# A third score buffer for the first batch of a hashed attention kernel, and the preparation work moved around it

## The chip, the cores and the metric

The kernel runs on one core of one Trainium2 chip. The metric is the device time of one execution in microseconds (us). The profile's span, from the first to the last instruction, is 1.7 to 1.9 us shorter in every execution of the kernel before. Engines are PE (TensorE matmul), PEld (its weight load), DVE (VectorE), ACT (ScalarE), POOL (GpSimd) and SP (SyncE); a name ending in q is an engine's issuing side. L290 is line 290 of the kernel that the trace belongs to, so the same code has different numbers before and after.

## The reference

Attention in which a query sees only keys of the same hash bucket (six sign bits of a projection), then a layer `h * cos(h)` between two matrices.

```python
# q, k, v: (4, 8, 768, 64)   proj: (64, 6)   w_in: (512, 2048)   w_out: (2048, 512)
q_bits = (einsum('bhsd,dk->bhsk', q, proj) > 0)      # k_bits likewise
mask   = q_bucket[:, :, :, None] == k_bucket[:, :, None, :]   # bucket = the bits as a number
scores = where(mask, q @ k.T / sqrt(64), -1e9)
attn   = softmax(scores)                             # denominator + 1e-9
x      = (attn @ v) -> (3072, 512)                   # heads side by side
h      = x @ w_in
out    = (h * cos(h)) @ w_out
```

## The kernel before

The mask costs no separate step: Q and K get six further rows of signs times a constant, so that one matmul gives score plus bonus for equal bits, and an exp with a fixed bias makes the rest vanish. A *unit* is one head and one block of 128 keys: two score matmuls, one exp on ScalarE, six value products. There are 48 units in a batch and 192 in all. After unit 55 comes the first layer of batch 0, after 103 that of batch 1, and so on. Batches 1 to 3 have the second layer of an earlier batch to fill TensorE between units (`fill`); batch 0 has nothing.

Two heads are a *pair*, 16 pairs in all. Each needs, ahead of its first score: loads, casts (GpSimd), block transposes (VectorE), the hash (TensorE), signs, and Q and K with tokens along the free dimension. Pairs 0 to 4 get the last by TensorE transposes and copies out of an output bank; the others by a transposing transfer that gives Q, and a VectorE copy (`k_copy`) that moves K to its own tile.

```python
s_ps = [psp.tile([P, 2, 512], FP32, name=f"s_ps{i}") for i in range(2)]   # two scores, 2 banks each
av_ps = [psp.tile([P, 512], FP32, name=f"av_ps{i}") for i in range(2)]    # two value banks
m_ps = [psp.tile([P, 512], FP32, name=f"m_ps{i}") for i in range(2)]      # two output banks
...
def score(h, jt):
    sp = s_ps[state["rot"] % 2]
    ...                                   # two matmuls, then the exp
def kc(n=n):
    k_copy(n, 0); k_copy(n, 1); bits_dma(n, (0, 1, 2, 3))
...
# preparation of pair n (n >= 5), s0 = 12 * (n - 1) - 6 (pair 5: - 4)
at(s0 - 1, lambda n=n: load(n + 1, nc.gpsimd))      # pairs 7 to 14
at(s0, start)       # casts, block transposes
at(s0 + 2, hsh)     # transposing transfers
at(s0 + 3, hsh2)    # hash, signs, bit rows (pair 5: s0 + 5)
at(s0 + 7, kc)      # K copies, bit rows to Q and K
...
for u in range(U):
    score(h, jt); pend.append((h, jt))
    ...  av_step()                        # value products; after a head's last: normalisation
    for f in acts.get(u, ()): f()         # the preparation placed at unit u
    ...  fill(UF(u))
```

The order in the program is each engine's order. What matters later: `kc` at unit 121 comes *behind* that unit's value products, and so behind the normalisation of the head that ends there.

The softmax here doesn't subtract the row's maximum and nothing guards it: scores larger than these inputs give would overflow.

Of the kernel before, what the change touches and what calls it, by code (L numbers as in the profile page):

```python
# [9 lines left out]
FP32 = mybir.dt.float32  # L10
# [12 lines left out]
def kernel(  # L23
# [31 lines left out]
    GDEF = range(2)  # L55
    COOL = False

    glob = ctx.enter_context(tc.tile_pool(name="glob", bufs=1))
# [21 lines left out]
    warm = glob.tile([P, 1], FP32, name="warm")  # L80
    wz = glob.tile([P, 512], FP16, name="wz")
    proj2 = glob.tile([32, 2, NBITS], FP32, name="proj2")
    projblk = glob.tile([P, 2, 4, 8], FP32, name="projblk")
# [6 lines left out]
    vs_bufs = [glob.tile([P, 2, W], FP16, name=f"vs{i}") for i in range(3)]  # L90

    s_ps = [psp.tile([P, 2, 512], FP32, name=f"s_ps{i}") for i in range(2)]
    av_ps = [psp.tile([P, 512], FP32, name=f"av_ps{i}") for i in range(2)]
    m_ps = [psp.tile([P, 512], FP32, name=f"m_ps{i}") for i in range(2)]
    state = {"m": 0, "rot": 0, "hold": False, "cool": False}

# [48 lines left out]

    def blocks(pr, hh=None):
        if pr not in blk:
            blk[pr] = [blkp.tile([P, 2, T, 2, 32], FP32, name=nm) for nm in ("blkq", "blkk")]
        for w in range(2):
            if hh is None:  # L150
                nc.vector.transpose(  # L151
                    out=blk[pr][w].rearrange("p h t c r -> p (h t c r)"),
                    in_=nat[pr][w].rearrange("p h f -> p (h f)"))
            else:
                nc.vector.transpose(
                    out=blk[pr][w][:, hh].rearrange("p t c r -> p (t c r)"),
                    in_=nat[pr][w][:, hh])
# [87 lines left out]
    pts = {}  # L245

    def score(h, jt):
        pr, hh = divmod(h, 2)
        sp = s_ps[state["rot"] % 2]
        state["rot"] += 1  # L250
        for c, (c0, c1) in enumerate(((0, 512), (512, 768))):
            nc.tensor.matmul(  # L252
                out=sp[:, c, 0:c1 - c0],
                lhsT=kx(pr)[:, hh, jt * P:(jt + 1) * P],
                rhs=qx(pr)[:, hh, c0:c1],
                start=True, stop=True)
        pt = ptp.tile([P, S], FP16, name="pt")
        nc.scalar.activation(  # L258
            out=pt, in_=sp.rearrange("p c n -> p (c n)")[:, 0:S], func=ACTF.Exp,
            bias=exp_bias, scale=EXP_SCALE)  # L260
        pts[(h, jt)] = pt

    def av(h, jt):
        pr, hh = divmod(h, 2)
        bank = av_ps[h % 2]
        if jt == 0 and h < DPE:
            nc.tensor.matmul(
                out=bank[:, 0:T * W].rearrange("p (t w) -> p t w", w=W)[:, :, 0:D + 1],
                lhsT=delta_w,
                rhs=vs_bufs[pr % 3][:, hh, 0:D + 1].unsqueeze(1).to_broadcast([P, T, D + 1]),  # L270
                start=True, stop=False, skip_group_check=True)
        elif jt == 0:
            nc.tensor.matmul(
                out=bank[:, T * W:T * W + D + 1], lhsT=delta_w, rhs=vs_bufs[pr % 3][:, hh, 0:D + 1],
                start=True, stop=False, skip_group_check=True)
        pt = pts.pop((h, jt))
        for qt in range(T):
            nc.tensor.matmul(  # L278
                out=bank[:, qt * W:qt * W + D + 1],
                lhsT=pt[:, qt * P:(qt + 1) * P],  # L280
                rhs=vx_bufs[pr % 3][:, hh, jt, 0:D + 1],
                start=False, stop=(jt == T - 1 and qt == T - 1), skip_group_check=True)

# [25 lines left out]
    def xtrans(b, ft):  # L309
        xT[(b, ft)] = xtp.tile([P, T, P], FP16, name=f"xT{ft}")  # L310
        nc.sync.dma_start_transpose(
            out=xT[(b, ft)], in_=xn[(b, ft)].rearrange("p t w d -> p (t w d)"))

    g_tiles = {}
# [83 lines left out]
    def av_step():  # L398
        ph, pj = pend.pop(0)
        av(ph, pj)  # L400
        if pj == T - 1:
            norm(ph)
            if ph % 2 == 1:
                xtrans(ph // H, (ph % H) // 2)

    def warmup(n):
        for _ in range(n):
            nc.tensor.matmul(  # L408
                out=s_ps[1][:, 1, :], lhsT=wz[:, 0:P], rhs=wz, start=True, stop=True,
                skip_group_check=True)  # L410

    with tc.manual_schedule():

        nat[0] = [natp.tile([P, 2, T * D], FP32, name=nm) for nm in ("natq", "natk", "natv")]
        aps = [heads_ap(src, 0) for src in (q, k, v)]
        nc.scalar.dma_start(out=proj2, in_=proj.rearrange("(c p) i -> p c i", c=2))
        nc.sync.dma_start(out=nat[0][0][:, 0], in_=aps[0][:, 0])
        nc.scalar.dma_start(out=nat[0][1][:, 0], in_=aps[1][:, 0])
        nc.sync.dma_start(out=nat[0][0][:, 1], in_=aps[0][:, 1])
        nc.sync.dma_start(out=nat[0][1][:, 1], in_=aps[1][:, 1])  # L420
        nc.scalar.dma_start(out=nat[0][2], in_=aps[2])
        load(1, nc.sync)
        load(2, nc.sync)
        nc.vector.memset(wz, 0.0)
        nc.vector.memset(exp_bias, EXP_BIAS)
        nc.vector.memset(cos_bias, math.pi / 2.0)
        nc.vector.memset(projblk, 0.0)
        nc.vector.memset(bitrow, 2.0 * BIT)
# [12 lines left out]
        warmup(8)  # L441
        for b_ in range(4):
            nc.vector.tensor_copy(
                out=projblk[32 * b_:32 * b_ + 32, :, b_, 0:NBITS], in_=proj2)
        blocks(0, 0)
        cast_qk(0, 0, (nc.scalar, nc.scalar))
# [10 lines left out]
        warmup(1)  # L457
        rows_copy(nc.vector, pe_transposes(0, 0, 1, av_ps[0]))
        rows_copy(nc.scalar, pe_transposes(0, 0, 0, m_ps[0], range(0, 3)))
        rows_copy(nc.vector, pe_transposes(0, 0, 0, m_ps[1], range(3, 6)))  # L460
        blocks(0, 1)
# [9 lines left out]
        U = 2 * NP * T  # L471
        L1_AT = {UB * b + 7: b - 1 for b in range(1, B)}
        acts = {}

        def at(u, f):
            acts.setdefault(u, []).append(f)

        at(0, second_a)
        at(1, second_b)
        for w_ in range(2):  # L480
            at(2 + w_, lambda w_=w_: rows_copy(nc.vector, pe_transposes(0, 1, w_, m_ps[w_])))
        for n in range(1, NP):
            s0 = 12 * (n - 1) - (0 if n < NEARLY else 4 if n == NEARLY else 6)
            def start(n=n):
                cast_qk(n, None, (nc.gpsimd, nc.gpsimd))
                blocks(n)
                cast_v(n)
            if n < NEARLY:
                at(s0 + 2, lambda n=n: load(n + 2, nc.sync if n + 2 < NEARLY else nc.gpsimd))
            elif NEARLY + 1 < n < NP - 1:  # L490
                at(s0 - 1, lambda n=n: load(n + 1, nc.gpsimd))
            if n < NEARLY:
                o_ = 3 if n == 1 else 0
                held = {}
                def hash_a(half, n=n, held=held):
                    ts = range(3 * half, 3 * half + 3)
                    held["bh"] = hash_sums(
                        n, m_ps[half], [(j % 2, j // 2, ts) for j in range(4)],
                        held.get("bh"), 3 * half)
                def hash_b(n=n, held=held):  # L500
                    token_bits(n, held["bh"], m_ps[0])
                def trp(hh, w, n=n):
                    rows_copy(nc.vector, pe_transposes(n, hh, w, m_ps[1 - w]))
                at(s0 + o_, start)
                for half in range(2):
                    at(s0 + 3 + o_ + half, lambda hash_a=hash_a, half=half: hash_a(half))
                at(s0 + 5 + o_, hash_b)
                for i in range(4):
                    at(s0 + (6 if n == 1 else 7) + o_ + i, lambda trp=trp, i=i: trp(i // 2, i % 2))
            else:  # L510
                def hsh(n=n):
                    dma_transposes(n, 0)
                    dma_transposes(n, 1)
                def hsh2(n=n):
                    hash_mm(n, m_ps[1 - state["m"]])
                def kc(n=n):
                    k_copy(n, 0)
                    k_copy(n, 1)
                    bits_dma(n, (0, 1, 2, 3))
                at(s0, start)  # L520
                at(s0 + 2, hsh)
                at(s0 + (5 if n == NEARLY else 3), hsh2)
                at(s0 + 7, kc)
        for i in range(4):
            at(6 + 8 * i, lambda i=i: weights_in(i))

        done = 0
        for u in range(U):
            h, jt = divmod(u, T)
            score(h, jt)  # L530
            pend.append((h, jt))
            for _ in range(2):
                if len(pend) > (4 if u < T else 2):
                    av_step()
            for f in acts.get(u, ()):
# [4 lines left out]
            if u in L1_AT:  # L540
                bb = L1_AT[u]
                state["hold"] = bb > 0
                for ff in range(NFF):
# [8 lines left out]
                    if bb == 0:  # L552
# [5 lines left out]
                        elif ff == NFF // 2:  # L558
                            load(NEARLY + 2, nc.gpsimd)
                    if ff in AVS[bb > 0] and len(pend) > 0:  # L560
                        av_step()
# [49 lines left out]
```

## Time and profile before

| | before |
|---|---|
| time, median of 3 | 310.24 us (310.15 to 310.26) |
| first exp | 9.26 us |
| end of the batch-0 exps (start of the cosine table load) | 59.86 us |
| attention of batch 1, of batch 2 (between table loads) | 44.74, 44.56 us |
| K copies waiting for transposing transfers, whole span | 0.7 us |

ScalarE loads a table whenever it turns from exp to cosine or back, so the starts of those loads cut the span into stages. I compare stages so throughout. The lines of the profile are in the prediction below. Read the busy share of TensorE (97%) with suspicion, and the timeline of ScalarE in batch 0 as the real account: each new row there is a gap.

### The profile page before, as it was taken

The page shows a single profiled execution, that of the slowest core. Times are in us where ns is not written, and L with a number is a line of the kernel's source. Part 1 is how long each engine was busy: PE and PEld are TensorE (multiplying, and loading weights), DVE is VectorE, ACT ScalarE, POOL GpSimd, SP SyncE. Part 2 cuts the span into 40 slices and gives each one's busy share as a digit, 9 for nine tenths or more (in the row PEclk, how much of TensorE's full clock was granted, in tenths as well). Part 3 has the DMA queues.
Part 4 walks back from the last instruction along what each step waited for, and adds up shares of the span by engine and source line. Part 5 has one row for each costly group of instructions (what it writes and reads, how often), then busy time and mean ns, then how long its engine had stood idle before and what let it go on. Part 6 is the DMA issues. An engine that isn't in the chain of part 4 may idle for free.

```text
span 308.4 us, 7711 instructions
## 1 busy us (share of the span) xinstructions
PE 300.1 (97%) x3090; PEld 182.8 (59%) x3090; DVE 201.8 (65%) x434; ACT 234.3 (76%) x288; POOL 109.4 (35%) x180
## 2 busy tenths in 40 slices
PE   8899999899999999999999999999999999999995
PEld 3577677556566666555566666555566664565444
DVE  3665466877598988866777878766777343577211
ACT  3788999977899999766899999766899993577000
POOL 4898258378384684400064584100030000000000
PEclk9999999999999999999999999999999999999998
DMA  6969969289469856700169979200133223100121
GB/s 205 376 109 163 333 86 214 33 140 192 163 172 268 215 162 168 217 2 0 45 80 234 234 146 199 48 18 2 53 62 89 68 62 94 36 0 0 62 76 69
DMA packets 45332, 37.74 MB, mean 122 GB/s; under 512 B 32264, under 2 KB 39200, under 8 KB 45296
## 3 DMA queue, kind: packets, MB, share of 16 engines
q1 hardware_dynamic: 38080, 19.35, 28.9%
q0 software_dynamic: 6576, 17.17, 21.0%
q10 hardware_dynamic: 640, 0.72, 0.7%
q8 instruction: 24, 0.39, 0.5%
q14 instruction: 12, 0.10, 0.1%
HBM read 27.26 MB, written 6.29 MB: 109 GB/s over the span
## 4 chain that ended last, share of the span: by engine, by line
PE 89%; ACT 6%; DVE 3%; issue 1%; ACTq 0%; DVEq 0%
PE m_ps L370 26%; PE s_ps L320 18%; PE s_ps L252 18%; PE av_ps L278 10%; PE m_ps L320 6%; ACT pt L258 5%; PE m_ps L164 4%; PE av_ps L320 2%; PE s_ps L408 1%; PE m_ps L354 1%; PE m_ps L224 1%; DVE g L337 1%; DVE blkq L151 1%; ACT cos L332 1%; PE av_ps L164 1%
## 5 line engine op out<-in xcount | busy, mean ns | idle before, releaser
L258 ACT ACTIVATE pt<-s_ps,exp_bias 128x768 f16<-128x768 f32 x192 | 161.7, 899 | 11.1 <-PE s_ps L252 9.7
L370 PE MATMUL m_ps<-wout,g 128*128 128x512 f16 x368 | 105.6, 379 | 0.1
L252 PE MATMUL s_ps<-qx,kx 128*128 128x512 f16 (+1 forms) x384 | 93.8, 326 | 2.6 <-ACT pt L258 1.2
L278 PEld LDWEIGHTS <-pt 128*128 128x128 f16 x1152 | 58.7, 97 | 21.7
L320 PEld LDWEIGHTS <-win 128*128 128x128 f16 x512 | 50.0, 98 | 34.6 <-issue 0.2
L278 PE MATMUL av_ps<-vx,pt 128*128 128x65 f16 x1152 | 65.7, 193 | 0.0
L320 PE MATMUL s_ps<-xT,win 128*128 128x384 f16 x352 | 62.3, 326 | 0.1
L337 DVE TENSOR_TENSOR g<-s_ps,cos 128x768 f16<-128x768 f32 x44 | 42.1, 958 | 28.1 <-ACT cos L332 28.1
L332 ACT ACTIVATE cos<-s_ps,cos_bias 128x768 f16<-128x768 f32 x44 | 39.7, 901 | 26.8 <-PE s_ps L320 25.4
L252 PEld LDWEIGHTS <-kx 128*128 128x128 f16 x384 | 35.2, 97 | 31.1 <-issue 3.3
L138 POOL CAST vx<-natv 128x768 f16<-128x768 f32 x16 | 13.3, 829 | 92.8 <-PE av_ps L278 87.8
L370 PEld LDWEIGHTS <-g 128*128 128x128 f16 x368 | 31.2, 98 | 20.1 <-issue 3.3
L376 DVE COPY ob<-m_ps 128x512 f32<-128x512 f32 x23 | 15.8, 686 | 22.6 <-PE m_ps L370 22.6
L320 PE MATMUL m_ps<-xT,win 128*128 128x384 f16 x120 | 27.6, 326 | 0.0
L332 ACT ACTIVATE cos<-m_ps,cos_bias 128x384 f16<-128x384 f32 x30 | 16.3, 578 | 7.0 <-PE m_ps L320 7.0
L305 DVE TENSOR_TENSOR xn<-tot,rc 128x384 f16<-128x384 f32 x24 | 20.1, 839 | 0.8
L337 DVE TENSOR_TENSOR g<-m_ps,cos 128x384 f16<-128x384 f32 x30 | 15.7, 550 | 1.3 <-ACT cos L332 1.0
L300 DVE COPY dv<-av_ps 128x65 f32<-128x65 f32 x24 | 5.1, 211 | 16.9 <-PE av_ps L278 16.9
L140 POOL TENSOR_TENSOR vhalf<-natv 128x384 f32<-128x384 f32 x16 | 15.9, 996 | 0.0
L133 POOL CAST n16x<-natq 128x768 f16<-128x768 f32 (+1 forms) x16 | 13.1, 822 | 5.1 <-DMA natq<-in_q_dram 5.1
L133 POOL CAST n16x<-natk 128x768 f16<-128x768 f32 (+1 forms) x16 | 13.0, 813 | 5.5 <-DMA natk<-in_k_dram 5.5
L151 DVE STREAM_TRANSPOSE blkq<-natq 128x768 f32<-128x768 f32 x15 | 14.6, 975 | 0.3
(77 smaller groups left out, 274.8 us busy)
## 6 DMA issues: line engine op xcount, KB each, us to landing
out_dram<-ob SPq DMA_DIRECT2D x23, 256.0 KB
natq<-in_q_dram POOLq DMA_DIRECT2D x11, 384.0 KB, 3.9
natk<-in_k_dram POOLq DMA_DIRECT2D x11, 384.0 KB, 4.7
natv<-in_v_dram POOLq DMA_DIRECT2D x11, 384.0 KB, 5.7
win<-in_moe_w_in_dram POOLq DMA_DIRECT2D x4, 512.0 KB, 7.3
wout<-in_moe_w_out_dram POOLq DMA_DIRECT2D x16, 128.0 KB, 5.1
natq<-in_q_dram SPq DMA_DIRECT2D x4, 384.0 KB
natk<-in_k_dram SPq DMA_DIRECT2D x4, 384.0 KB
```

The source lines that it names most:

```text
L133: engs[w].tensor_copy(out=o_, in_=i_)
L140: nc.gpsimd.tensor_tensor(out=half, in0=nv[:, :, 0:3, :], in1=nv[:, :, 3:6, :], op=ALU.add)
L151: nc.vector.transpose(out=blk[pr][w].rearrange("p h t c r -> p (h t c r)"), in_=nat[pr][w].rearrange("p h f -> p (h f)"))
L252: nc.tensor.matmul(out=sp[:, c, 0:c1 - c0], lhsT=kx(pr)[:, hh, jt * P:(jt + 1) * P], rhs=qx(pr)[:, hh, c0:c1], start=True, stop=True)
L258: nc.scalar.activation(out=pt, in_=sp.rearrange("p c n -> p (c n)")[:, 0:S], func=ACTF.Exp, bias=exp_bias, scale=EXP_SCALE)
L278: nc.tensor.matmul(out=bank[:, qt * W:qt * W + D + 1], lhsT=pt[:, qt * P:(qt + 1) * P], rhs=vx_bufs[pr % 3][:, hh, jt, 0:D + 1], start=Fal ...
L305: nc.vector.tensor_tensor(out=dst, in0=tot[:, :, 0:D], in1=rc.unsqueeze(2).to_broadcast([P, T, D]), op=ALU.mult)
L320: nc.tensor.matmul(out=halves[c][:, 0:C2], lhsT=win_t[ft][:, ff * P:(ff + 1) * P], rhs=xT[(b, ft)][:, 3 * c:3 * c + 3, :], start=(ft == 0) ...
L332: nc.scalar.activation(out=c_, in_=h_, func=ACTF.Sin, bias=cos_bias, scale=1.0)
L337: nc.vector.tensor_tensor(out=g_, in0=h_, in1=c_, op=ALU.mult)
L370: nc.tensor.matmul(out=o_ps, lhsT=g[:, qt * P:(qt + 1) * P], rhs=wout_t[ff], start=(ff == 0), stop=(ff == NFF - 1))
L376: nc.vector.tensor_copy(out=ob, in_=o_ps)
```

## The change

The intent: in batch 0 nobody uses the output banks except hashes and transposes. If those go to the value bank that is idle at the time, the two output banks can be a third score buffer until the first layer, and TensorE may run one exp ahead. To fit this in, the preparation is placed by hand, in half units (a half unit means: ahead of that unit's value products). From unit 15 to 46 the value products also run three units behind the scores instead of two (`LAG`). The rest is a faster start and moved loads. The core of the diff:

```diff
+    third = psc.tile([P, 2, 512], FP32, name="s_ps2")     # released before the first layer
+    s_ps.append(third)
...
     def score(h, jt):
-        sp = s_ps[state["rot"] % 2]
+        if h * T + jt == N3:                               # N3 = 15
+            ...
+        sp = s_ps[state["rot"] % (2 if h * T + jt < N3 else len(s_ps))]
...
-            if ph % 2 == 1:
+            if ph % 2 == 1 and ph != H - 1:
                 xtrans(ph // H, (ph % H) // 2)
...
-        nc.scalar.dma_start(out=proj2, in_=proj...)        # and four copies to projblk
+        for b_, eng in enumerate((nc.scalar, nc.sync, nc.scalar, nc.sync)):
+            eng.dma_start(out=projblk[32 * b_:32 * b_ + 32, :, b_, 0:NBITS], in_=proj...)
...
-                at(s0 - 1, lambda n=n: load(n + 1, nc.gpsimd))      # s0 = 12 (n-1) - 6
+                at(s0 - 5, lambda n=n: load(n + 1, nc.gpsimd))      # s0 = 12 (n-1)
...
-                at(s0, start); at(s0 + 2, hsh); at(s0 + 3, hsh2); at(s0 + 7, kc)
+                units = LATE.get(n, [s0 - 6 + d_ for d_ in (0, 2, 3, 6.5)])   # start, hsh, hsh2, kc
+            if n % 4 == 2 and n > NEARLY + 1:
+                ...                        # casts, blocks, transfers inside the layer
+                at(s0 - 4 + HS, hsh2); at(s0 - 1.5, kc)
+        at(XPE, lambda: xtrans_pe(0, NFT - 1, av_ps[(H - 1) % 2]))  # last block of batch 0 by TensorE
...
+            for f in acts.get(u - 0.5, ()): f()            # ahead of the value products of u
```

In the same units as before: the loads were placed one unit ahead of the casts of the pair before, and are now one unit behind them; the K copies of pairs 8, 11, 12 and 15 were at a full unit (121 for pair 11) and are now half a unit earlier (120.5); those of pairs 10 and 14 are 2.5 units earlier, and those of pairs 9 and 13 now stand inside a first layer.

## The prediction

> **What bounds the kernel now.** I read three views in this order: the page (shares and slices), the chain of waits for the whole span, and the timeline of ScalarE and VectorE for the first 60 us. The program has one odd stage. Batch 0 (48 units of score, exp and value product, then the first output layer, which starts after unit 55) has no output-layer work of an earlier batch to fill TensorE with. Every later stage has.
>
> ```profile
> PE 300.1 (97%) x3090; PEld 182.8 (59%) x3090; DVE 201.8 (65%) x434; ACT 234.3 (76%) x288; POOL 109.4 (35%) x180
> ...
> PE   8899999899999999999999999999999999999995
> ...
> ACT  3788999977899999766899999766899993577000
> ...
> L258 ACT ACTIVATE pt<-s_ps,exp_bias 128x768 f16<-128x768 f32 x192 | 161.7, 899 | 11.1 <-PE s_ps L252 9.7
> ```
>
> A TensorE busy share of 97% would leave nothing to win, but it hides the first stage: matmul ends are modelled, so a matmul that sits behind a wait looks like work. The chain separates the two. In the first batch it keeps passing to exps and back; from 59.10 on it is almost only TensorE:
>
> ```profile
> 40.82 0.80 ACT pt L258
> 41.67 0.65 ACT pt L258
> 42.47 0.90 ACT pt L258
> 43.41 0.49 PE s_ps L252 x2
> 44.87 0.47 PE m_ps L164 x16
> 45.95 0.47 PE m_ps L164 x16
> 47.90 0.48 PE s_ps L252 x2
> ...
> 58.13 0.93 ACT pt L258
> 59.10 1.46 PE s_ps L320 x8
> ...
> 283.98 17.27 PE m_ps L370 x80
> 301.24 3.51 PE m_ps L354 x32
> ```
>
> To test that "almost only", I add up TensorE work in a stretch of batch 1, 83 to 125 us: 47 score pairs at 0.325 us, 70 output-layer matmuls at 0.216, 276 value products at 0.030, four hashes at 0.79, seven denominators at 0.03 make 42.1 us of 42.0. The six other stretches to 304.8 agree within 0.5 us each. So about 246 us of the span are dense TensorE work that this change doesn't shorten. What can shrink is the time before 59.1 us.
>
> The timeline of ScalarE gives that stage unit by unit (start, length, group):
>
> ```profile
> 9.26 0.90 ACT L258 ACTIVATE pt<-s_ps,exp_bias 128x768 f16<-128x768 f32 x1 [0.77 <-PE s_ps L252]
> 10.66 4.86 ACT L258 ACTIVATE pt<-s_ps,exp_bias 128x768 f16<-128x768 f32 x6 [0.51 <-PE s_ps L252]
> 15.97 0.90 ACT L258 ACTIVATE pt<-s_ps,exp_bias 128x768 f16<-128x768 f32 x1 [0.44 <-PE s_ps L252]
> 17.23 7.05 ACT L258 ACTIVATE pt<-s_ps,exp_bias 128x768 f16<-128x768 f32 x8 [0.36 <-PE s_ps L252]
> 24.83 0.90 ACT L258 ACTIVATE pt<-s_ps,exp_bias 128x768 f16<-128x768 f32 x1 [0.55 <-PE s_ps L252]
> 25.91 10.19 ACT L258 ACTIVATE pt<-s_ps,exp_bias 128x768 f16<-128x768 f32 x12 [0.18 <-PE s_ps L252]
> 36.60 10.17 ACT L258 ACTIVATE pt<-s_ps,exp_bias 128x768 f16<-128x768 f32 x12 [0.50 <-PE s_ps L252]
> 46.95 7.58 ACT L258 ACTIVATE pt<-s_ps,exp_bias 128x768 f16<-128x768 f32 x9 [0.18 <-PE s_ps L252]
> 54.98 4.86 ACT L258 ACTIVATE pt<-s_ps,exp_bias 128x768 f16<-128x768 f32 x6 [0.45 <-PE s_ps L252]
> ```
>
> Those are 56 exps, units 0 to 55. The last row has six in 4.86 us, so five intervals and one length of 0.90: (4.86-0.90)/5 = 0.79 us per exp. That is the floor, with nothing but score and value product on TensorE. The rows of twelve run at (10.19-0.90)/11 = 0.845, and between rows there are gaps of 0.2 to 0.55. Unit 15 starts at 17.23+7*0.879 = 23.4, unit 55 at 58.94: 35.5 us for 40 intervals, 0.89 each.
>
> **What the Trainium skill says.** "ScalarE: Activation LUTs", section "What ACT_TABLE_LOAD costs", gives about 280 ns + 0.833 ns per element for an activation with a pointer bias, less about 93 ns when back to back. For 768 elements that is 920 and 827 ns; the trace has 899 and 790, and the trace is used. "PSUM — Partial Sum Buffer", section "Specifications (TRN2)": eight banks of 2 KiB per partition. This kernel has all eight allocated (two score tiles of two, two value banks, two output banks), so a third score buffer must take the output banks; the diff does just that. "Perfetto Trace Analysis", section "Identifying the Most-Contended Engine", warns that matmul busy share doesn't show distance from the limit; the 97% above, beside 0.10 us lost per exp, agrees. "TensorE: Matmul & The Clock Gate", Part 1: slow clock until some 3.4 us of activity. Here warm-up matmuls of 512 columns are issued 0.43 us apart at first, against 0.216 later.
>
> **The change part by part.**
>
> *Start.* The projection goes by four small transfers directly to its block form; four copies (0.70 us on VectorE) fall away, and the first half of K is issued some 0.45 us earlier. Before: second transpose of the first head at 4.47, hash at 5.11, first score at 8.72. VectorE could end that transpose 0.35 earlier, and the first score then waits for a K copy of 128 columns instead of 768 (0.56 us, perhaps 0.2 now). I expect the first exp at about 8.5 instead of 9.26, 0.75 earlier. But this doesn't carry through. The listing of the changed program puts half of pair 1's block transposes (2 x 0.55 us) ahead of the copies of the second head (2 x 0.56), and the other half (1.1) behind them. Following VectorE: first-head copies to 8.4, transposes to 9.5, hash, signs and bits to 11.2, transposes to 12.3, two copies with TensorE transposes between to 13.95, transposes to 15.05. The hash of pair 1 then starts near 15.1, against 14.84 before. It is now one hash of 0.79 us instead of two of 0.47 a unit apart, with still only two score buffers, so unit 7 waits for all of it. From there I get unit 15 at about 23.6, against 23.4. Effect: -0.2 us, uncertain by 0.6.
>
> *Third score buffer, units 15 to 55.* TensorE work of these 40 intervals: 41 scores x 0.33 plus 0.1 after each hash or bit step (the chain shows 0.43 there) = 14.1; 41 value products x 0.18 = 7.4; six denominators x 0.17 = 1.0; hashes of pairs 2 to 5, 4 x 0.79 = 3.2; bits 3 x 0.26 = 0.8; 78 transposes x 0.058 = 4.5. Sum 31.0 us. ScalarE: 40 x 0.79 = 31.6. Both are close to full, and with two buffers each long TensorE unit costs ScalarE its excess: score 0.43 + product 0.18 + half hash 0.47 = 1.08 against 0.79. With three, TensorE may be about one exp late before ScalarE notices. The worst run, a hash unit (excess 0.61), a bits unit (0.08) and a transpose unit (0.18), is 0.87 us together, about what the third buffer absorbs. So these intervals should fall from 0.89 to close to the floor; with some 0.02 us per unit for waits on VectorE copies I take 0.81: 40 x 0.81 = 32.4, a gain of 3.1 us.
>
> *Hash and transposes into the idle value bank.* Same work; 24 transposes in three groups of eight instead of four of six. The bank must be copied out before the next head's first product. Most groups stand two or more units (1.6 us) ahead of that, while a copy group takes 0.8. No gain of its own: it frees the banks.
>
> *Entry to the output layer.* With three buffers in rotation the layer takes the tile of unit 53, not 54, so its first matmuls may start one exp earlier. The fourth tile must wait for table load (1.28), cosine (0.90) and product (0.96) after the last exp, 3.15 us; before it was reached 3.53 us after. Gain 0.4. Six TensorE transposes and a copy replace the last transposing transfer; before it was issued at 54.5, uncomfortably close to a shorter stage.
>
> *Later batches.* Casts, block transposes and loads are moved into the output layers. TensorE does the same work and was dense; perhaps 0.3 us of waits vanish.
>
> Sum: -0.2 + 3.1 + 0.4 + 0.3 = 3.6 us: 306.6. Hand-set half-unit positions look like a schedule tuned with care, and my start stage is a pessimistic hand count, so I shift by 0.5: 306.1 us.
>
> **Rivals.** (1) TensorE becomes the bound of the first batch. For: 31.0 against 31.6 us. If waits for sign and copy steps add 1.5 us, the interval is 0.85 and the gain of that part 1.5: about 308. (2) Loads bind. For: between 25 and 40 us the DMA share is above 1.0, and pair 4's K and V landed at 37.3 and 41.7, waiting behind weights and pair 5. Against: its issue stood behind the transposing transfer at 24.41, itself behind block transposes of 1.8 us on VectorE that are now split and moved; it should issue about 4 us earlier. If it binds, the blocks of pair 4 wait at unit 33 and the total is 307 to 309. (3) Start and middle both reach the floor: units 0 to 15 at 0.79 from 8.5 gain 3 us, and the sum is 7: 303. Against: the serial VectorE chain above.
>
> **Range and chances.** Two percent is 6.2 us, below 304.0. That needs rival 3 mostly true, while the middle alone can't give more than 35.5-31.6 = 3.9. I take 304.2 to 308.2; faster by over 2%: 0.11, within 2%: 0.86, slower: 0.03.
>
> **What would show it.** First output-layer matmul at 55 to 56 us instead of 59.1; the rest from there to the end within 1 us of the 249 us of before; exps of units 15 to 55 at 0.79 to 0.83; unit 15 no earlier than 23; first exp near 8.5; TensorE transposes just ahead of the layer. I am wrong if unit 15 comes a microsecond or more earlier (start misjudged), if exps stay at 0.85 or above with waits on copies of the value bank (rival 1) or on landings (rival 2), or if the part after the first layer changes by over 1 us.

## The result, and the profile after

| | before | after, first profile | after, second profile |
|---|---|---|---|
| time | 310.24 median | 308.96 median (308.37 to 309.13) | 308.31 median, six runs |
| profiled execution: time, span | 310.2, 308.4 | 308.96, 305.7 | 309.11, 307.3 |
| first exp | 9.26 | 9.61 | 9.22 |
| end of the batch-0 exps | 59.86 | 57.76 | 57.71 |
| from there to the end of the layer's cosines | 21.36 | 21.26 | 21.25 |
| attention of batch 1 | 44.74 | 44.69 | 44.69 |
| attention of batch 2 | 44.56 | 44.57 | 46.25 |
| from the last exp-to-cosine turn but one to TensorE's end | 109.66 | 109.66 | 109.65 |
| K copies waiting for transposing transfers | 0.7 | 6.0 | 8.7 |

The ratio is 0.9955, with a 95% interval of 0.9932 to 0.9978. A ratio is the mean time of one kernel's runs over that of the other's of the same rounds, so not quite the ratio of the medians quoted. Executions over 1.5% slower than the fastest of the same kernel are left out of the means. The change gained 1.3 us where I had expected 4.1, and the time fell outside the range.

The first profile has a span 3.3 us shorter than its time, against 1.7 to 1.8 in the two other runs (spans 307.4 and 306.6). So it doesn't show all of what the clock counted. It also shows no loss in batch 2 (44.57). For the later stages I read the second profile, of the same kernel run again, because the loss is in that one.

The page of the kernel after, busy shares, slices and the exp group:

```profile
PE 299.4 (98%) x3032; PEld 180.4 (59%) x3032; DVE 197.6 (65%) x447; ACT 233.1 (76%) x288; POOL 109.2 (36%) x184
...
PE   7999999999999999999999999999999999999995
...
ACT  3789999977899999766899999766899993577000
...
L290 ACT ACTIVATE pt<-s_ps,exp_bias 128x768 f16<-128x768 f32 x192 | 160.8, 901 | 9.8 <-PE s_ps L284 8.7
```

The eights of TensorE in the first slices became nines, yet the first one fell to 7. The shares hardly moved; they can't tell what was won. The timeline of ScalarE can (first profile; start, length, group; in brackets the idle time before):

```profile
9.61 4.23 ACT L290 ACTIVATE pt<-s_ps,exp_bias 128x768 f16<-128x768 f32 x5 [1.12 <-PE s_ps L284]
...
16.84 0.90 ACT L290 ACTIVATE pt<-s_ps,exp_bias 128x768 f16<-128x768 f32 x1 [0.85 <-PE s_ps L284]
...
19.15 17.31 ACT L290 ACTIVATE pt<-s_ps,exp_bias 128x768 f16<-128x768 f32 x21 [0.24 <-PE s_ps L284]
36.61 21.13 ACT L290 ACTIVATE pt<-s_ps,exp_bias 128x768 f16<-128x768 f32 x26
57.76 1.28 ACT L375 ACT_TABLE_LOAD   x1
```

Two things are to be seen. From unit 9 on, 47 exps run on end: (57.74 - 19.15 - 0.90)/46 = 0.82 us each, so the third buffer does what it should. But the first exp starts at 9.61 instead of the predicted 8.5.

For that start, TensorE's timeline, first of the kernel before, then after in its first profile (L408 and L451 are warm-up matmuls, L224 and L240 the transposes of the first head):

```profile
1.19 3.59 PE L408 MATMUL s_ps<-wz 128*128 128x512 f16 x8 [1.19 <-DVE cos_bias L426]
...
5.90 0.61 PE L408 MATMUL s_ps<-wz 128*128 128x512 f16 x1
...
6.69 0.39 PE L408 MATMUL s_ps<-wz 128*128 128x512 f16 x1
7.31 0.49 PE L224 MATMUL av_ps<-ident,n16x 128*128 128x128 f16 x6 [0.23 <-DVE n16x L203]
```

```profile
0.78 3.57 PE L451 MATMUL s_ps<-const-bfloat16-1.0 128*128 128x512 bf16 x8 [0.78 <-PEq L679]
5.18 0.34 PE L180 MATMUL av_ps<-blkq,projblk 128*32 128x96 f32 x1 [0.83 <-DMA projblk<-in_proj_dram]
...
5.98 0.61 PE L451 MATMUL s_ps<-const-bfloat16-1.0 128*128 128x512 bf16 x1
...
6.78 0.61 PE L451 MATMUL s_ps<-const-bfloat16-1.0 128*128 128x512 bf16 x1
...
7.45 0.84 PE L240 MATMUL s_ps<-ident,n16x 128*128 128x128 f16 x6
```

The eight warm-ups end at 4.35, but the hash waits until 5.18 for the projection. After it, both single warm-up matmuls take 0.61 us, where before only the first did and the second took 0.39; and six transposes take 0.84 instead of 0.49. So TensorE, which in the kernel before is at full pace by the second of them, is still near half of it at the transposes. I call this half clock below. The page's clock row shows 9 here all the same, so it has to be read from durations. The packed trace says why: its record of the granted clock has no entry before full clock is granted, which is at 6.48 us in the kernel before, at 9.72 in this profile and at 8.55 in the second one, and the page takes the time without an entry as full.

The table of waits gives the other finding. The columns are who waits, for what, us in total, times, longest. Before:

```profile
POOL n16x L133 <- DMA natq<-in_q_dram: 5.1, 2, 3.9
...
DVE kx L243 <- DMA qx<-n16x: 0.7, 2, 0.4
```

After, second profile:

```profile
POOL n16x L149 <- DMA natq<-in_q_dram: 15.3, 7, 4.1
DVE kx L259 <- DMA qx<-n16x: 8.7, 4, 4.0
```

Casts now wait for their own loads, and VectorE's K copies for transposing transfers. The first kind costs nothing where GpSimd has slack; whether the second does is read from the chain of waits. Second profile after, where batch 2 loses its time:

```profile
171.79 0.79 PE m_ps L180 x16
172.57 0.18 PE m_ps L413
172.76 6.96 DMA qx<-n16x
179.72 0.02 issue
179.75 0.62 DVE kx L259
180.37 0.15 DVE dv L334
...
181.36 0.56 DVE xn L339
181.92 0.60 DVE ob L419
182.52 0.89 DVE blkq L167
183.41 0.87 DVE blkk L167
184.28 0.04 issue
184.32 0.85 PE m_ps L180 x14
```

Between 168 and 196 us the chain of the kernel before is nothing but TensorE. Here it leaves TensorE at 172.76 for a transfer, runs through six kinds of VectorE work that stand behind the K copy, and comes back only with the next hash (L180).

### The profile page after: what moved, and what is told of

Its sections match the earlier page's. It is cut to its first block, busy times and chain, and to the rows that moved or that the text cites. A ratio compares the mean times of both kernels' runs of the same rounds, so it can differ in the third digit from the quotient of the medians.

```text
span 305.7 us, 7617 instructions
## 1 busy us (share of the span) xinstructions
PE 299.4 (98%) x3032; PEld 180.4 (59%) x3032; DVE 197.6 (65%) x447; ACT 233.1 (76%) x288; POOL 109.2 (36%) x184
## 4 chain that ended last, share of the span: by engine, by line
PE 91%; ACT 3%; DVE 2%; issue 1%; DMA 1%; SPq 0%; DVEq 0%; ACTq 0%
PE m_ps L413 26%; PE s_ps L284 19%; PE s_ps L363 17%; PE av_ps L311 11%; PE m_ps L363 6%; PE m_ps L180 3%; PE av_ps L363 2%; PE av_ps L180 2%; ACT pt L290 2%; PE av_ps L550 1%; PE m_ps L397 1%; DMA projblk<-in_proj_dram 1%; DVE g L380 1%; ACT cos L375 1%; PE av_ps L214 1%
## 5 line engine op out<-in xcount | busy, mean ns | idle before, releaser
L311 PEld LDWEIGHTS <-pt 128*128 128x128 f16 x1152 | 57.8, 97 | 21.5 <-ACT pt L290 1.6
L284 PEld LDWEIGHTS <-kx 128*128 128x128 f16 x384 | 33.9, 97 | 27.5 <-issue 1.2
L640 POOL COPY mark<-g 128x1 f16<-128x1 f16 x4 | 0.8, 190 | 51.0 <-DVE g L380 51.0
L339 DVE TENSOR_TENSOR xn<-tot,rc 128x384 f16<-128x384 f32 x24 | 16.3, 678 | 0.8
L259 DVE COPY kx<-qx 64x768 f16<-64x768 f16 x22 | 10.0, 492 | 6.4 <-DMA qx<-n16x 6.0
```

Source lines behind the costliest of these rows:

```text
L284: nc.tensor.matmul(out=sp[:, c, 0:c1 - c0], lhsT=kx(pr)[:, hh, jt * P:(jt + 1) * P], rhs=qx(pr)[:, hh, c0:c1], start=True, stop=True)
L311: nc.tensor.matmul(out=bank[:, qt * W:qt * W + D + 1], lhsT=pt[:, qt * P:(qt + 1) * P], rhs=vx_bufs[pr % 3][:, hh, jt, 0:D + 1], start=(h ...
L339: nc.vector.tensor_tensor(out=dst, in0=tot[:, :, 0:D], in1=rc.unsqueeze(2).to_broadcast([P, T, D]), op=ALU.mult)
```

## The experiments

Fifteen runs were made, each beside the kernel before on the same chip.

### Which part does what: the changed kernel again, old projection load, two buffers, longer warm-up

Four runs of one set; the kernel before took 310.18 in the median of eleven.

**The changed kernel again**, no edit.

> The changed kernel once more, for its spread and as the partner of the other three of this set. From its first runs: 308.4 to 309.1 us against 310.2, with spans between 305.7 and 307.4. If the spread comes from the clock of TensorE in the first ten microseconds, spans of different runs differ by up to 1.7 us while the kernel before stays within 0.3.

Measured 308.31 (307.84 to 310.29), ratio 0.9939 [0.9907, 0.9970]. Its profile is the second one above. It runs over 2.4 us from execution to execution, where most runs of the kernel before stay within 0.5: something in it is decided anew each time.

**Old projection load**: one small transfer ahead of K, then four VectorE copies.

```diff
+        nc.scalar.dma_start(out=proj2, in_=proj.rearrange("(c p) i -> p c i", c=2))
-        for b_, eng in enumerate((nc.scalar, nc.sync, nc.scalar, nc.sync)):
-            eng.dma_start(out=projblk[32 * b_:32 * b_ + 32, :, b_, 0:NBITS], ...)
+        for b_ in range(4):
+            nc.vector.tensor_copy(out=projblk[32 * b_:32 * b_ + 32, :, b_, 0:NBITS], in_=proj2)
```

> The changed kernel with the projection loaded as before: one small transfer ahead of K, four copies on VectorE. Theory A (the direct load of the projection is what lost the start: it landed at 5.04 us, 3.36 us after its issue, TensorE idled 0.83 us before the first hash and then ran its transposes and first scores at half clock, 0.105 us per transpose instead of 0.058): hash near 4.8 to 5.1 without a gap, transposes at 0.058, first exp near 8.7 instead of 9.61, total 0.7 to 1.5 us below the changed kernel, and less spread. Rival B (the start doesn't reach the end, VectorE's chain of transposes and copies absorbs it): same as the changed kernel within 0.3.

Measured 308.83 (307.63 to 310.51), ratio 0.9949 [0.9920, 0.9978]; first exp in its profile at 9.95. So the old load does not bring the start back. The block transpose of K waits 0.75 us for K, and the warm-ups, which the change also lets start 0.4 us earlier, are over before that: warm-up matmuls 0.61, transposes at half clock. The theory that the direct projection alone costs the start fell. What the two starts share is a gap of some 0.8 us between the warm-ups and the end of the hash. That the gap is the cause is not shown: two later profiles had a gap and full clock (0.72 us with loads first, 1.49 us with all K copies later, where the hash ran at full clock and the granted clock then fell to 0.50 between 8 and 10 us).

**Two score buffers throughout**, all else as changed.

```diff
-        if h * T + jt == N3:
-            ...
-        sp = s_ps[state["rot"] % (2 if h * T + jt < N3 else len(s_ps))]
+        sp = s_ps[state["rot"] % 2]
```

> The changed kernel with two score buffers in rotation throughout; the third tile serves the transposes only, as it does anyway in the first 15 units. Theory A (the third buffer carries the gain): units 15 to 55 at 0.86 to 0.89 us instead of 0.82, total 2 to 3.5 us above the changed kernel, so above the kernel before as well, 310.5 to 312. Rival B (the new placing of hashes and transposes carries it, the buffer little): within 1 us of the changed kernel.

Measured: ratio 1.0050 [1.0019, 1.0082]; four runs from 310.85 to 312.69, two over 317. The timeline of ScalarE:

```profile
26.42 8.47 ACT L285 ACTIVATE pt<-s_ps,exp_bias 128x768 f16<-128x768 f32 x10 [0.45 <-PE s_ps L279]
35.34 9.37 ACT L285 ACTIVATE pt<-s_ps,exp_bias 128x768 f16<-128x768 f32 x11 [0.45 <-PE s_ps L279]
45.16 10.06 ACT L285 ACTIVATE pt<-s_ps,exp_bias 128x768 f16<-128x768 f32 x12 [0.45 <-PE s_ps L279]
```

A gap of 0.45 us returns once per pair, at the hash, and the batch-0 exps end at 60.56 instead of 57.71. That is 2.85 us for the third buffer, with the longer lag of the value products in place in both. It also shows that the change without its third buffer would have lost time.

**Longer warm-up**: `warmup(8)` became `warmup(12)`.

> The changed kernel with 12 warm-up matmuls ahead of the first hash instead of 8. They cover the wait for the projection, which still lands near 5.0. If the half clock is what costs (not the late landing itself): no idle before the hash, transposes at 0.058 instead of 0.105, first exp about 0.6 to 0.9 us earlier than 9.61, total 0.5 to 1 below the changed kernel. If the landing itself is the loss: hash still at 5.2, total the same within 0.3.

Measured 313.17 (310.54 to 314.22), ratio 1.0081 [1.0045, 1.0116]: slower, against expectation. The start itself worked, in part: TensorE is at full clock, which its timeline shows.

```profile
0.78 5.04 PE L451 MATMUL s_ps<-const-bfloat16-1.0 128*128 128x512 bf16 x12 [0.78 <-PEq L679]
...
6.91 0.39 PE L451 MATMUL s_ps<-const-bfloat16-1.0 128*128 128x512 bf16 x1
...
7.58 0.50 PE L240 MATMUL s_ps<-ident,n16x 128*128 128x128 f16 x6
```

Twelve delay the hash to 5.8 us, so the first exp is at 9.07 only, and the batch-0 exps end 0.4 us earlier than in the second profile. But batch 2 took 50.18 us, against 44.56 in the kernel before and 46.25 in the second profile after. Four more warm-ups, some 1.5 us of TensorE's time at the start, went with a median 4.9 us longer than the changed kernel's. So the loss in batch 2 is a matter of when things meet, and no longer a detail of one profile. In this profile the clock added to it: TensorE was busy for only 0.21 us of the stretch from 170 to 172 us, and its granted clock was 0.67 in the next 2 us and 0.50 in the 2 us after that. The chain there has a transposing transfer of 11.53 us, and the K copies wait 12.9 us in total.

### What makes the transfers late: the order of loads

In the chain above, the couple's first transfer was issued at 171.26 (the chain shows its second, of 172.76), 3.15 us behind a load of 1.2 MB issued on the GpSimd queue. The change had put the loads of pairs 8, 9, 12 and 13 behind the casts, and a cast of V waits for a free value buffer, so loads come late and near the transfers. Three kernels ask whether this is the cause, and a fourth whether the last block of batch 0 needs TensorE. The kernel before took 310.25 here.

**Loads ahead of the casts again**, all else as changed.

```diff
-                at(s0 - 5, lambda n=n: load(n + 1, nc.gpsimd))
+                at(s0 - 7, lambda n=n: load(n + 1, nc.gpsimd))
```

> The changed kernel with the loads of pairs 8, 9, 12 and 13 put back ahead of the casts of the pair before (two units earlier, as in the kernel before). Theory C (GpSimd's queue is in order; the change put the load behind a V cast that waits for a free value buffer, so it is issued one pair later, just ahead of its own casts; the transposing transfer, VectorE's K copy and TensorE then wait for it): batch 2's attention, from the last cosine of its first output layer to the next, takes 44.6 us as before instead of the 46.3 to 50.2 of four of five profiles; casts no longer wait for natq; total 307.0 to 307.8 and little spread. Rival D (the transposing transfers are slowed by something else, such as the order of bits and output transfers on their queue): waits of the K copy for the transposing transfer stay at 7 to 13 us, total 308.3 or more.

Measured 307.18 (306.76 to 307.56), ratio 0.9892 [0.9868, 0.9916]; batch 2 took 44.60, though K copies still waited 3.7 us. It looked like the answer. In this profile the start happened to be warm with eight warm-ups, which took 3.44 us instead of 3.57 and were followed by 0.72 us without work (first exp at 8.54):

```profile
0.78 3.44 PE L451 MATMUL s_ps<-const-bfloat16-1.0 128*128 128x512 bf16 x8 [0.78 <-PEq L679]
...
7.05 0.49 PE L240 MATMUL s_ps<-ident,n16x 128*128 128x128 f16 x6
```

So eight are enough in some executions and not in others.

**The same with ten warm-ups** (`warmup(10)`).

> The run before this one with 10 warm-up matmuls instead of 8, which end near 5.0 us, when the projection lands. Twelve gave full clock for the transposes and first exp at 9.07, but held the hash to 5.81. Theory: hash at 5.2, transposes at 0.058 us, first exp near 8.6 to 8.9, end of batch 0's exps 0.5 to 0.9 us earlier than 57.7, total 0.5 to 0.9 below the run without. Rival: the clock needs the longer warm-up, or VectorE's chain absorbs it; then equal within 0.3.

Measured: 306.85, 306.88, 308.54, 308.97, 309.16 and 309.86, ratio 0.9931 [0.9897, 0.9965]. The start was as hoped (transposes x6 in 0.50 us, first exp at 8.56), but in the profiled run batch 2 took 46.33 again, with a K copy that waited 4.61 us. So the loads' order alone is not the cause.

**The kernel before with its loads behind the casts** (`at(s0 - 1, load)` became `at(s0 + 1, load)`).

> The kernel before with one edit: each later load moved two units, from one unit ahead of the casts of the pair before it to one unit behind them. Theory C: this alone brings the loss, loads issued a pair later, casts waiting for natq, K copies waiting for the transposing transfers, 1 to 6 us more than the kernel before, with spread. Rival D: within 0.5 us of it.

Measured 310.32 (309.88 to 312.73), ratio 0.9989 [0.9965, 1.0013]. Casts waited 23.3 us for Q, more than four times as long as before, no K copy waited, and batch 2 still took 44.57. The profiled run was the 312.73, which lost at its start: TensorE was slow there too (transposes 0.85, first exp at 10.70), so this happens to the kernel before as well, if seldom. So late loads don't hurt a kernel whose K copies stand where they stood before. The run does not test a load that comes closer to a transfer: the loads stood 3.6 to 4.1 us ahead of it, as in the kernel before (3.6 to 4.1).

**The second of these with the last block of batch 0 by a transfer**, as before the change.

```diff
-            if ph % 2 == 1 and ph != H - 1:
+            if ph % 2 == 1:
...
-        at(XPE, lambda: xtrans_pe(0, NFT - 1, av_ps[(H - 1) % 2]))
```

> The second run of this set, but with the last feature block of batch 0 transposed by a transfer as before, instead of six TensorE transposes and a copy. Theory (that transfer would be too late for the shorter first batch): it is issued near 52, lands 3 to 5 us later, and the first output layer's last accumulation waits: first layer 0.3 to 1.5 us later. Rival (it still lands in time): 0.1 to 0.4 us faster than with TensorE, as the transposes fall away.

Measured 306.59 (306.39 to 306.80), ratio 0.9873 [0.9846, 0.9899]. Its profiled execution took 1731 us, with the first ten matmuls in 13.23 us instead of 4.43, and tells nothing. The kernel was run again later.

> The fastest kernel so far once more (loads ahead of the casts, 10 warm-ups, last block by a transfer, K copies early as in the change), because its profile fell into an odd execution of 1731 us. If it is sound: again 306.4 to 306.8. If its four runs were luck: a spread like that of its sibling, 306.9 to 309.9.

Measured 306.95 (306.46 to 307.09), ratio 0.9871 [0.9838, 0.9904]; first layer matmul at 55.91 us, batch 2 44.56. The odd execution didn't come back and stays unexplained. In this profile the layer is not held up by the transfer, and both runs are as fast as any: the six TensorE transposes are not needed. The K copies still waited 5.0 us here, and why these runs are steady and those of their sibling with TensorE transposes (306.85 to 309.86) are not is not settled.

### The K copies' place in VectorE's order

In the kernel before, VectorE does the normalisation first and comes to the K copy afterwards (timeline of VectorE, before):

```profile
178.35 0.23 DVE L300 COPY dv<-av_ps 128x65 f32<-128x65 f32 x1 [1.52 <-PE av_ps L278]
178.61 0.56 DVE L301 TENSOR_TENSOR tot<-av_ps,dv 128x390 f32<-128x390 f32 x1
...
179.44 1.15 DVE L305 TENSOR_TENSOR xn<-tot,rc 128x384 f16<-128x384 f32 x1
180.96 0.35 DVE L243 COPY kx<-qx 64x768 f16<-64x768 f16 x1 [0.38 <-DMA qx<-n16x]
```

The transfer was issued at 174.52 and landed at about 180.9, 6.4 us later. VectorE turned to the copy at 180.58, 6.1 us after the issue, and so waited 0.4 us. In the second profile after, VectorE turns to the copy at 174.98, only 3.7 us after the issue:

```profile
178.95 0.35 DVE L259 COPY kx<-qx 64x768 f16<-64x768 f16 x1 [3.97 <-DMA qx<-n16x]
```

Half a unit is about 0.47 us of the stage's time (44.7 us for 48 units, halved), but in VectorE's order it jumps the wait for the value products (1.52) and the whole normalisation (2.2): 3.7 us. Landing times, for the first transfer of such a couple, the longest of some profiles:

| profile | load issued ahead of the transfer by | issue to landing |
|---|---|---|
| loads first | no load near | 3.7 or less |
| loads first, ten warm-ups | no load near | 3.4 |
| before | 4.05 us | 6.4 |
| after, second profile | 3.15 us | 7.7 |
| loads first | 1.61 us | 7.0 |
| loads first, ten warm-ups | 1.28 us | 9.7 |
| twelve warm-ups | 1.24 us | 11.5 |

This table picks long ones. Counted over all such couples after batch 0, in all sixteen profiles but the odd one: with a load issued less than 3.5 us ahead, 5.0 to 11.5 us (18 couples); with 3.5 to 4.2 us ahead, 3.5 to 7.0 us (38); with no load in the last 7 us, 2.5 to 4.7 us (63). So a load close ahead goes with a longer transfer, but 4 us ahead it can also make no difference. For couples within 4.2 us of a load the kernel before has room of about 6 us, the changed one in these profiles mostly 3.1 to 5.1 us. Five kernels test it.

**All the K copies later**: those of pairs 8, 11, 12, 15 by half a unit and those of 10 and 14 by 2.5 units, so all at their old place. (The kernel before took 310.19 in this set.)

```diff
-                units = LATE.get(n, [s0 - 6 + d_ for d_ in (0, 2, 3, 6.5)])
+                units = LATE.get(n, [s0 - 6 + d_ for d_ in (0, 2, 3, 7)])
-                at(s0 - 1.5, kc)
+                at(s0 + 1, kc)
```

> The changed kernel with only the K copies and bit transfers of the later pairs put back where the kernel before has them (half a unit later, behind the value products; 2.5 units later for pairs 10 and 14), loads as the change has them. Theory E (what slows a transposing transfer is the load it meets: with the bit transfers out of the way, SyncE issues the transposes of the next pair some 2.7 units earlier, 1.2 to 2.1 us behind a load of 1.2 MB instead of 4 us behind it; those with the shortest lead landed last): the transposes go out 3 or more us behind the load, the K copy waits under 2 us, batch 2's attention takes 44.6 us, total 306.9 to 307.8. Theory C (the loads' order on GpSimd is what counts, as putting it back gave 307.2): as the changed kernel, 308.3 to 309, with casts still waiting 14 us for natq.

Measured 308.45 (308.04 to 309.71), ratio 0.9945 [0.9919, 0.9972]. The K copies' waits went from 8.7 to 0.9 us, and yet batch 2 took 45.18. Its chain says why:

```profile
156.90 1.04 DVE kx L259 x2
157.93 0.61 DVE ob L419
...
159.54 4.93 DMA kx<-br
164.47 0.05 issue
164.52 0.50 PE s_ps L284 x2
```

Behind the copy go the bit rows, by small transfers. With the copy of pair 10 so late, its bits land when the first score of that pair is already due. The wait moved from one transfer to another: I had expected the loss to vanish, and it did not. The 2.5 units of pairs 10 and 14 belong to their later hash and should stay.

**Both, on top of the best kernel so far** (loads first, ten warm-ups, last block by a transfer).

> All repairs together: loads ahead of the casts, K copies where the kernel before has them, 10 warm-ups, last feature block transposed by a transfer. If the causes are found, every run is at 306.0 to 306.8, none above 307.5, and each profile has batch 2's attention at 44.6 us. The run of this kind without the later K copies had 306.4 to 306.8, but its sibling with TensorE transposes 306.9 to 309.9.

Measured 308.12 (307.06 to 308.39), ratio 0.9916 [0.9891, 0.9940], batch 2 45.38: worse than without, for the same reason. A miss too.

**The kernel before with the K copies early**: half a unit for 8, 11, 12, 15 and 2.5 for 10 and 14, nothing else.

```diff
-                at(s0 + 7, kc)
+                at(s0 + (7 if n < NEARLY + 3 or n % 4 == 1 else 4.5 if n % 4 == 2 else 6.5), kc)
...
+            for f in acts.get(u - 0.5, ()): f()
```

> The kernel before with the K copies of pairs 8 and up moved as the change moves them (half a unit earlier, pairs 10 and 14 by 2.5), nothing else. Theory E: the order on SyncE flips here too, but this kernel's transposes also wait for casts that stand behind the load on GpSimd, so they can still be some 3 us behind it; loss of 0 to 2 us in batch 2. If 2 us or more, the flip alone is the cause; if nothing, it needs the earlier casts of the change as well.

Measured: three runs at 312.22, 312.35 and 313.62, three slow ones over 317, ratio 1.0074 [1.0040, 1.0107]. The K copies wait 13.1 us, batch 2 takes 46.61. Early K copies produce the loss without anything else of the change.

Three runs then separated the half unit from the 2.5 units (the kernel before took 310.58 in this set). **The changed kernel with the half unit taken back alone**:

```diff
-                units = LATE.get(n, [s0 - 6 + d_ for d_ in (0, 2, 3, 6.5)])
+                units = LATE.get(n, [s0 - 6 + d_ for d_ in (0, 2, 3, 7)])
```

> The changed kernel with one number put back: K copies of pairs 8, 11, 12 and 15 half a unit later, so that they stand behind the normalisation of the head that has just ended on VectorE, not ahead of it. Pairs 10 and 14, and the loads, stay as the change has them. Theory F (the half unit is the loss: the K copy waits for the transposing transfer with the normalisation, the eviction and the block transposes behind it, and the next hash waits for those): no waits of TensorE for block transposes, batch 2's attention 44.6 us, total 307.0 to 307.8. Theory C (the order of the loads is needed too): 308 to 309.

Measured 307.72 (306.36 to 308.53), ratio 0.9896 [0.9861, 0.9931]. Batch 2 took 44.56 in its profile, no K copy waits, and casts wait 14.7 us for Q, as in the changed kernel. VectorE's timeline now has the old order:

```profile
177.48 1.14 DVE L339 TENSOR_TENSOR xn<-tot,rc 128x384 f16<-128x384 f32 x1
178.65 1.03 DVE L259 COPY kx<-qx 64x768 f16<-64x768 f16 x2
179.61 0.68 DVE L419 COPY ob<-m_ps 128x512 f32<-128x512 f32 x1
```

The copies (issue of the transfer at 172.55, 6.1 us ahead) have no bracket: no wait. One constant, 6.5 to 7, took the waits away although the loads are still late. That it took the loss away is likely, but these runs alone don't show it: the first profile of the changed kernel had no loss in batch 2 either, and the two kernels' intervals overlap (0.9907 to 0.9970 for the changed one).

**The kernel before with that half unit alone**, pairs 8, 11, 12, 15:

```diff
-                at(s0 + 7, kc)
+                at(s0 + (7 if n < NEARLY + 3 or n % 4 in (1, 2) else 6.5), kc)
...
+            for f in acts.get(u - 0.5, ()): f()
```

> The kernel before with only the half unit: K copies of pairs 8, 11, 12 and 15 ahead of the normalisation; pairs 10 and 14 stay. With both the kernel before lost 2.0 to 7.2 us. Theory F: a loss of at least 1.5 us stays. If the 2.5 units of pairs 10 and 14 were the loss: within 0.7 of the kernel before.

Measured 313.44 median of six (310.73 to 315.79), ratio 1.0063 [1.0017, 1.0108]. K copies wait 9.4 us. Its profile is of the fastest run and has 45.30 in batch 2; the loss is there, and spread at least as widely as in the changed kernel. One of its couples of transfers shows that a K copy can wait though its transfer takes no longer than before. It is issued at 163.38 and lands after 4.8 us, as in the kernel before (issued at 163.61, 4.7 us), but VectorE turns to it after 2.3 us instead of 6.1:

```profile
168.16 1.62 DVE L243 COPY kx<-qx 64x768 f16<-64x768 f16 x2 [2.46 <-DMA qx<-n16x]
```

How much wait is free can be read across the ten profiles with early K copies. Where the longest single wait of a K copy was 2.1 to 2.6 us (changed kernel's first profile, loads first, last block by a transfer), batch 2 took 44.56 to 44.60. Where it was 3.5 us or more, batch 2 took 45.30 to 50.18.

### The best of it

**Loads first, ten warm-ups, last block by a transfer, and the half unit taken back**: the changed kernel with four small edits, all shown above.

> That kernel with the half unit put back as in the first run of this set. Theory F: at most 306.8 in every run, no K copy ahead of a normalisation, so no run of 308 and more. If the bits' transfers then come too late, as in the run with all K copies late: 307 to 308.4.

Measured 306.76 (306.56 to 307.29), ratio 0.9870 [0.9840, 0.9900], span 304.8. It is faster than both kernels and among the steadiest of the variants. The timeline of ScalarE:

```profile
8.60 4.30 ACT L290 ACTIVATE pt<-s_ps,exp_bias 128x768 f16<-128x768 f32 x5 [0.64 <-PE s_ps L284]
...
18.32 38.59 ACT L290 ACTIVATE pt<-s_ps,exp_bias 128x768 f16<-128x768 f32 x47 [0.35 <-PE s_ps L284]
56.93 1.28 ACT L375 ACT_TABLE_LOAD   x1
```

The first exp comes at 8.60, the batch ends at 56.93, and batch 2 takes 44.56. Between this kernel and its twin without the half unit (306.95) there is no difference that the intervals would show. The twin's K copies still wait 5.0 us, but none of its ten sound executions lost by it, so that the half unit helps there is not shown.

## Why the prediction was wrong, and where it was right

Each step of the sum against the second profile, whose time is 309.11, in us gained over before:

| step of the prediction | predicted | measured |
|---|---|---|
| start, to unit 15 | -0.2 | -0.6 (unit 15 at about 24.0) |
| third buffer, units 15 to 55 | +3.1 | +2.7 (0.82 each, not 0.81; with two buffers 2.85 less) |
| entry to the output layer | +0.4 | +0.1 |
| later batches | +0.3 | -1.6 here; batch 2 alone 0 to -5.6 over all profiles with early K copies |
| after TensorE's last matmul | not considered | +0.5 (3.7 to 3.2 us) |
| shift for a "schedule tuned with care" | +0.5 | no ground for it |

The measured terms add up to the 1.1 us between the spans and times of the two profiled executions. The first profile, of the runs that gave the result, gains 2.1 us to the end of the exps, 0.1 in the layer, nothing lost later and 0.5 at the end, 2.7 us of span in all; there 1.5 us of the shortfall lie outside the span and stay unexplained. The other two of these three runs have longer spans (307.4 and 306.6), but no profile.

**The third buffer: right.** 47 exps on end, and TensorE did not become the bound (the first rival): the intervals are 0.82, not 0.85. Loads (the second rival) made the blocks of one pair wait 2.6 us on VectorE, but the unbroken row of exps shows that nothing came of it.

**Start: right in the serial part, wrong in its beginning.** I put unit 15 at 23.6 and the first exp at 8.5. The VectorE order did hold units 2 to 8 back, with the predicted wait of unit 7 for a whole hash (0.84 us). But I took the projection as off the path and TensorE as warm. The projection landed at 5.04, 3.4 us after its issue, and with eight warm-ups TensorE was still at half clock at the transposes in some executions. With ten warm-ups the first exp was at 8.56, 8.60, 9.00 and 9.07 in four profiles; in the first two, and with loads first, unit 15 came at 23.2 to 23.3.

**Entry: mis-sized.** The end of the exps and the fourth tile of the layer both moved by the same 2.1 to 2.2 us, so 0.1 was left of 0.4. The first layer matmul came at 56.4 where I had named 55 to 56.

**Later batches: the step that failed.** I wrote "TensorE does the same work and was dense; perhaps 0.3 us of waits vanish", and looked only at how much TensorE work there was. Measured in the second profile: batch 2 took 46.25 us instead of 44.56, 1.7 us lost where I had 0.3 gained, because VectorE stood before a K copy for 3.97 us. Without this loss the time would have been about 307.4 (an estimate, 309.11 less 1.7), and inside the range; the kernel with the half unit taken back alone had 307.7. I had listed the casts, block transposes and loads that move there, but not the half unit of the K copies, which the listing of VectorE's order shows. I also didn't compare what room a K copy had behind its transfer before (6.1 us) with what the transfer took (3.7 to 6.4 us where a load stood close). For one couple that room was used up in the kernel before already, and its 0.7 us of waits were the sign. Of the things that would make me wrong, I had named this one: that the part after the first layer changes by over 1 us.

What is shown: moving the half unit back removes the K copies' waits in the changed kernel (0 instead of 6.0 and 8.7 us); moving it forward in the kernel before makes the waits and a loss of time clear of noise (ratio 1.0063 [1.0017, 1.0108]). What is likely, but not clear of noise by itself: that the half unit is the whole loss of time in the changed kernel. What is only argued: that the load, rather than something else near it, stretches the transfer. The landing times go that way on the whole, with exceptions, and no run took the load away by itself. What stays open: what makes a transfer land late in one execution and not in the next, so that one loses nothing and another 4 us; the up to 1.5 us outside the span; the steadiness of the kernels whose last block goes by a transfer; and the one execution of 1731 us.

## What to carry to other kernels

Before moving an instruction on an in-order engine, count what it jumps there and how long the transfer it needs has been under way by then: a step of half a unit in the program was 3.7 us in VectorE's order. A stage that is "dense" before is no promise that it stays so: look there for waits that are short but not zero. And test a schedule in many executions, as a wait that depends on how transfers meet doesn't show in each of them.

## What the Trainium skill lacked or had wrong

- "TensorE: Matmul & The Clock Gate", Part 1, ties the clock to some 3.4 us of sustained activity and says that this varies from run to run. The runs agree that it varies, and show how much a start this short depends on it. The changed kernel and its variants with eight warm-ups (3.44 to 3.57 us, then 0.7 to 1.5 us of idle time ahead of or inside the hash) have seven profiles: in five the first head's six transposes took 0.84 to 0.85 us, in one 0.49, in one 0.55 with slow ones behind. With ten or twelve they took 0.49 to 0.50 in all five profiles, though in two with ten the hash just before was still slow. Full clock was granted between 3.96 and 9.72 us in these twelve profiles, where the first matmul starts at 0.78. The page's clock row doesn't show that time as slow.
- "DMA: Bandwidth & Descriptors", section "Latency and other measured facts", gives an effective rate for transposing transfers, but nothing on one that meets a bulk load: 2.5 to 4.7 us with no load issued in the 7 us before, 5.0 to 11.5 us when issued less than 3.5 us behind a load of 1.2 MB. The last of the projection's four transfers of 1.5 KB landed 3.0 to 3.9 us after its issue, more than the some 2 us that the page calls a fixed cost (and fits on transfers issued from GpSimd; these were issued from ScalarE and SyncE).
- No page that I found tells to look for what stands behind a waiting instruction on an in-order engine: here one K copy that waited 4.0 us held up normalisation, an eviction and two block transposes, until TensorE waited too.
